# TensorE's order written out and bound by dependencies in a gated-recurrence and maxout-FFN kernel

## The chip, the cores and the metric

The kernel runs on one core of a Trainium2 chip. The metric is the device time of one execution in microseconds (us). Most executions of one kernel agree within 1%.

## The reference, cut to what matters

A linear recurrence with a complex gate for each channel (4 batches, 8 heads, 768 steps, head size 48), whose output goes through a feed-forward block with a maximum of three projections.

```python
mag = np.sqrt(a_re * a_re + a_im * a_im)
scale = np.minimum(mag, 0.999) / (mag + 1e-06)        # gate, limited in size
...
for t in range(S):
    new_re = ar * S_re - ai * S_im
    new_im = ar * S_im + ai * S_re
    S_re, S_im = (new_re + kv, new_im)                # kv = k[t] outer v[t]
    y[:, :, t] = np.einsum('bhd,bhde->bhe', q[:, :, t], S_re)
...
h = np.maximum(np.maximum(x @ w1, x @ w2), x @ w3)    # 3072 x 384 by 384 x 768
return h @ w_out
```

## The kernel before

Tokens are taken in tiles of 128 and groups of two tiles; there are twelve groups. The names in the profile are these:

- Gates of the *next* group, in three steps on ScalarE, VectorE and GpSimd: logarithms of size (`Ln`) and half-angle tangents (`w`). ScalarE's table functions are bound to each other in the order in which the program emits them:

```python
def tab(ins):
    if "tab" in T:
        tc.add_manual_dep(ins.ins, T["tab"].ins.name, order, reason="table order")
    T["tab"] = ins

def act(**kw):
    tab(nc.scalar.activation(**kw))
...
def s2():                                             # the last gate step
    L, w, e, ar, ai = part("L"), part("w"), part("e"), part("ar"), part("ai")
    nc.scalar.activation(out=e, in_=ar, func=AF.Abs)
    nc.vector.tensor_tensor(out=w, in0=w, in1=e, op=OP.add)
    act(out=L, in_=w, func=AF.Ln)
    act(out=L, in_=L, func=AF.Exp, scale=-1.0)
    (nc.gpsimd if g > 1 else nc.vector).tensor_tensor(out=ai, in0=ai, in1=L, op=OP.mult)
    nc.vector.tensor_tensor(out=w, in0=w, in1=L, op=OP.mult)
    nc.vector.scalar_tensor_tensor(out=w, in0=w, scalar=2.0, in1=ai, op0=OP.subtract, op1=OP.mult)
    nc.scalar.activation(out=ar, in_=ar, func=AF.Sign, bias=tiny)
    nc.scalar.activation(out=ai, in_=ar, func=AF.Copy, scale=-0.25, bias=0.25)
    nc.scalar.activation(out=ar, in_=ar, func=AF.Copy, scale=-1.0 / math.pi)
```

- Angles: after two sums (`mds`, one a tile, each followed by two Exps and GpSimd's products into k and q) comes a table load, Arctan of `w`, two VectorE products, and the cumulative sums `cs` on TensorE; then sines.

```python
def turns(g, cs, meanwhile):
    act(out=w[:, lo:hi], in_=w[:, lo:hi], func=AF.Arctan)
    nc.vector.tensor_tensor(out=w[:, lo:hi], in0=w[:, lo:hi], in1=ar[:, lo:hi], op=OP.mult)
    nc.vector.tensor_tensor(out=w[:, lo:hi], in0=w[:, lo:hi], in1=ai[:, lo:hi], op=OP.add)
    meanwhile(2)                                      # two steps of the FFN
    for c in cs:
        ...
        nc.tensor.matmul(out=ps, lhsT=upto, rhs=w[:, c * DM:(c + 1) * DM], start=True, stop=c == 0)
```

- A tile: transposes (`tp`), factors of decay (`F`), products with them on VectorE (`Q`, `KB`, `QB`, `QG`), score products `A` and `B`, state products `dk`, suffix sums (`sfx`), outputs `y`. FFN: `up` and `op`.

The order of emission is woven from streams. The compiler's scheduler may then put the instructions of an engine in another order, as it does in e1 below:

```python
return [call(scores, x, "A"), call(gather, x, "A"), call(scores, x, "B")] + tr[:1] \
    + [call(gather, x, "B"), call(state, x)] + tr[1:] + ct + pr[:1] + kt \
    + [call(outputs, x, tokens(x))] + pr[1:]
...
weave((0.0, 1.0, tile_steps(g * C) + tile_steps(g * C + 1)), (0.0, 0.7, pre_steps(g + 1, feed)),
      (0.0, 1.0 if g > 1 else 0.5, [call(feed, 1) for _ in ffn]))
```

Of the kernel before, what the change touches and what calls it, by code (L numbers as in the profile page):

```python
# [45 lines left out]
def kernel(  # L46
# [52 lines left out]
# [5 lines that stand above are left out]

    def act(**kw):
        tab(nc.scalar.activation(**kw))  # L106

    def table(nm):
        tab(nc.scalar.preload_act_table_set(nm))
# [240 lines left out]
    def turns(g, cs, meanwhile):  # L350

        lo, hi = cs[0] * DM, (cs[-1] + 1) * DM
        w, ar, ai = T["w", g], flat(T["ar", g]), flat(T["ai", g])
# [3 lines that stand above are left out]
        meanwhile(2)  # L357
        for c in cs:
            ps = psM.tile([P, DM], FP, tag="mm", padded_shape=[P, 512], name="cs")
            nc.tensor.matmul(out=ps, lhsT=upto, rhs=w[:, c * DM:(c + 1) * DM], start=True, stop=c == 0)  # L360
            if c > 0:
                nc.tensor.matmul(out=ps, lhsT=every, rhs=w[:, 0:DM], start=False, stop=True)
            t = nat2.tile([P, DM], FP, tag="t", name="t")
            nc.scalar.activation(out=t, in_=ps, func=AF.Copy, bias=MAGIC)
            nf = nat2.tile([P, DM], FP, tag="nf", name="nf")
            nc.vector.scalar_tensor_tensor(out=nf, in0=t, scalar=MAGIC, in1=ps, op0=OP.subtract, op1=OP.subtract)
            T["nf", g * C + c] = nf
            if c == C - 1 and (g + 1) % GB > 0:
                T["carry", g + 1] = nat1.tile([1, DM], FP, tag="carry", name="carry")
                nc.scalar.dma_start(out=T["carry", g + 1], in_=nf[P - 1:P])  # L370
# [29 lines left out]
    def products(x):  # L400
        g, c = divmod(x, C)

        def sums(mat, nm):
            ps = psM.tile([P, DM], FP, tag="mm", padded_shape=[P, 512], name=nm)
            nc.tensor.matmul(out=ps, lhsT=mat, rhs=T["Ln", g][:, c * DM:(c + 1) * DM], start=True, stop=True)  # L405
            return ps

        def s0():

            ps = sums(mid, "mds")  # L410
            for nm, sg in (("k", 1.0), ("q", -1.0)):
                E = nat2.tile([P, DM], FP, tag="E", name="E")
                act(out=E, in_=ps, func=AF.Exp, scale=sg)
                eng = nc.gpsimd if g > 1 else nc.vector
                eng.tensor_tensor(out=hd(T[nm, x]), in0=E, in1=hd(T[nm, x]), op=OP.mult)  # L415

        def s1():
            for nm in "kq":
                u = T["U" + nm, x] = us[nm][x % len(us[nm])]
                nc.vector.tensor_tensor(out=u[:, :, :, 0:D], in0=T["CS", x], in1=two(hd(T[nm, x])), op=OP.mult)  # L420

        def s2():

            ps = sums(rest, "sfx")
            En = nat2.tile([P, DM], FP, tag="E", name="En")
            act(out=En, in_=ps, func=AF.Exp, scale=-1.0)
            u = T["Uk", x][:, :, :, 0:D]
            nc.vector.tensor_tensor(out=u, in0=u, in1=two(En), op=OP.mult)

        return s0, s1, s2  # L430


    def turn(x, hg):
        if hg == 0:
            T["K", x] = un2.tile([P, H, P], FP, tag="K", name="K")

            T["Q", x] = un2.tile([P, 4 * H, 48], FP, tag="Q", name="Q")
        hs = slice(hg * HU, (hg + 1) * HU)
        for nm in "kq":
            tp = psM.tile([P, HU, P], FP, tag="mm", padded_shape=[P, 4, P], name="tp")  # L440
            for j in range(HU):
                nc.tensor.transpose(out=tp[0:DD, j], in_=both(T["U" + nm, x], hg * HU + j), identity=ident)  # L442
            if nm == "k":
                nc.scalar.copy(out=T["K", x][0:DD, hs], in_=tp[0:DD])  # L444
            else:
                nc.scalar.copy(out=T["Q", x][0:DD, 4 * hg * HU:4 * (hg + 1) * HU, 0:32],
                               in_=tp[0:DD].rearrange("p j (c t) -> p (j c) t", c=4))

    def cut(x):
        g, c = divmod(x, C)  # L450
        F = T["F", x] = fs[x % 2]
        ps = psM.tile([P, HU, NF], FP, tag="mm", padded_shape=[P, 4, P], name="F")
        for h in range(H):
            o = h % 2 * L64
            nc.tensor.matmul(out=ps[o:o + D, h // 2], lhsT=T["Ln", g][:, c * DM + h * D:c * DM + (h + 1) * D],  # L455
                             rhs=cuts, start=True, stop=True)

        for o in (0, L64):
            for h in range(2):
                act(out=F[o:o + D].rearrange("p (i h) n -> p i h n", h=2)[:, :, h], in_=ps[h * L64:h * L64 + D],  # L460
                    func=AF.Exp, scale=-1.0)
# [35 lines left out]
    def scores(x, nm):  # L497

        ps = psS.tile([P, 2, 512], FP, tag="s", name=nm)
        for h in range(H):  # L500
            for o in range(0, P, 32):
                c, j = divmod(o // 32, 2)
                if nm == "A":
                    nc.tensor.matmul(out=ps[o:o + 32, 0, h * 48:(h + 1) * 48], lhsT=T["K", x][0:DD, h, o:o + 32],  # L504
                                     rhs=T["Q", x][0:DD, 4 * h + 2 * c + j], start=True, stop=True)
                else:
                    nc.tensor.matmul(out=ps[o:o + 32, h // HU, h % HU * P:h % HU * P + 80],  # L507
                                     lhsT=T["KB", x][0:DD, h, o:o + 32],
                                     rhs=T["QB", x][0:DD, 2 * h + c, 16 * j:16 * j + 80], start=True, stop=True)
        T[nm, x] = ps  # L510
# [28 lines left out]
    def state(x):  # L539
# [8 lines left out]
        for h in range(H):  # L548
            o = h % 2 * (P - D)
            for lo, hi in ((0, L64), (L64, DD)):  # L550
                for c in range(2):
                    r = slice(c * L64, (c + 1) * L64)
                    nc.tensor.matmul(out=ps[lo:hi, c, h * D:(h + 1) * D], lhsT=both(T["Uk", x], h)[r, lo:hi],  # L553
                                     rhs=T["v", x][r, c, h // 2, o:o + D], start=True, stop=True)
        dk = ps[0:DD, :, 0:DM].rearrange("p c (i u d) -> p c i u d", u=2, d=D)
        G = T["G", x]
# [9 lines left out]
    def outputs(x, xs):  # L566
# [10 lines left out]
        for todo in zip(*queues):  # L577
            for r, c, i, n, new, start, stop in todo:
                h, lo = 2 * i + n // 2, 32 * n
                nc.tensor.matmul(out=y[32 * (r % 4):32 * (r % 4) + 32, r // 4, c * L64:(c + 1) * L64],  # L580
                                 lhsT=V[:, c, i, lo:lo + 32] if new else G[0:DD, c, i, lo:lo + 32],
                                 rhs=atm[:, h] if new else QG[0:DD, 2 * h + c], start=start, stop=stop)
        if x == xs[0]:
# [7 lines left out]
    def up_step(xs, fp, i):  # L591
# [7 lines left out]
        for j in range(2):  # L599
            f = 2 * fp + j  # L600
            for d in range(KD):
                nc.tensor.matmul(out=ps[:, j], lhsT=ws[i][:, d, f * P:(f + 1) * P], rhs=xT[:, d],  # L602
                                 start=(d == 0), stop=(d == KD - 1))
        if i == 0:
            nc.scalar.copy(out=dst, in_=ps)  # L605
# [3 lines left out]
    def out_step(xs, x):  # L609
        hT, o = T["hT", xs[-1]], (x - xs[0]) * P  # L610
        ps = psM.tile([P, DM], FP, tag="mm", padded_shape=[P, 512], name="op")
        for f in range(KF):
            nc.tensor.matmul(out=ps, lhsT=hT[:, f, o:o + P], rhs=wo[:, f], start=(f == 0), stop=(f == KF - 1))  # L613
        ot = fp2.tile([P, DM], FP, tag="ot", name="ot")
        nc.scalar.copy(out=ot, in_=ps)  # L615
        nc.sync.dma_start(out=out[x * P:(x + 1) * P, :], in_=ot)


    def call(f, *a):
        return lambda: f(*a)  # L620
# [71 lines left out]
    load(2, load_a, load_kq)  # L692


    held = []
    for g in range(1, NG):
        load(g + 1, load_v)
        load(g + 2, load_a, load_kq)
        ffn = held + ffn_steps(tokens(g * C - 1))
        held = [ffn.pop()]  # L700

        def feed(n):
            for _ in range(min(n, len(ffn))):
                ffn.pop(0)()

        if g > 1:
            feed(1)
        weave((0.0, 1.0, tile_steps(g * C) + tile_steps(g * C + 1)), (0.0, 0.7, pre_steps(g + 1, feed)),
              (0.0, 1.0 if g > 1 else 0.5, [call(feed, 1) for _ in ffn]))
    for f in held + ffn_steps(tokens(NX - 1)):  # L710
        f()

# [29 lines left out]
```

## Time and profile before

| | |
|---|---|
| time | 724.0 us (median of 3; 722.6 to 724.2) |
| span of the profiled run | 719.9 us |
| granted TensorE clock, mean | 0.974 |
| TensorE, VectorE, ScalarE, GpSimd busy | 90%, 72%, 56%, 17% |
| first A of the third group to first A of the last, nine groups | 165.2 to 639.2 us, 52.7 us each |

A "group time" below is this distance. The prediction shows the lines and how they are read. In a line of the order of time, the first number is the start in us and the second the time from the first start to the last end; since matmuls overlap (in the prediction's lines 36 ups last 7.93 us, and the next matmul starts after 7.77), I take distances between starts. In a line of waits the numbers are: total us, times, longest.

### The profile page before, as it was taken

The numbers are of one execution on the slowest core, as the hardware profiler recorded it, in microseconds if no ns is written. First come the engines' busy times: TensorE is split into PE (matmuls) and PEld (weight loads), VectorE is DVE, ScalarE is ACT, GpSimd is POOL, SyncE is SP. The second block draws the span as 40 slices with busy tenths as digits, with TensorE's granted clock in tenths as the row PEclk, the third lists the DMA queues.
The fourth block names the chain that finished last, engine by engine and source line by source line (L and its number), as shares of the span: only waits on it lengthen the run. The fifth ranks groups of instructions, "written<-read, shape, count | busy, mean of one in ns | idle before, by whom it ended". The sixth has DMA issues, their size and how long they took to land.

```text
span 719.9 us, 22988 instructions
## 1 busy us (share of the span) xinstructions
PE 649.9 (90%) x10308; PEld 505.3 (70%) x10308; DVE 515.7 (72%) x718; ACT 400.3 (56%) x677; POOL 120.6 (17%) x121
## 2 busy tenths in 40 slices
PE   1256678779999999999999999999999999999997
PEld 0144567657877878878778778878778778778785
DVE  6999998867856867867856867867857858755210
ACT  6778665666556556556556656566466465422000
POOL 9300000601301302202203103104004004000000
PEclk9987799979999999999999999999999999999999
DMA  9780442040320320330320320410410210000000
GB/s 226 218 191 15 95 126 46 13 89 24 57 60 21 57 63 18 57 68 14 66 67 5 73 63 4 87 47 9 94 36 13 46 36 2 2 25 2 14 11 22
DMA packets 134178, 39.23 MB, mean 54 GB/s; under 512 B 126784, under 2 KB 129856, under 8 KB 134080
## 3 DMA queue, kind: packets, MB, share of 16 engines
q1 hardware_dynamic: 133824, 37.76, 23.7%
q8 instruction: 80, 1.31, 0.8%
q14 instruction: 18, 0.15, 0.1%
q10 hardware_dynamic: 256, 0.01, 0.0%
HBM read 33.03 MB, written 4.72 MB: 52 GB/s over the span
## 4 chain that ended last, share of the span: by engine, by line
PE 69%; issue 14%; DVE 8%; ACT 6%; DMA 2%; POOL 1%; SPq 0%; DVEq 0%; ACTq 0%; POOLq 0%
PE up L602 31%; PE op L613 13%; PE tp L442 5%; PE y L580 5%; PE dk L553 3%; PE B L507 2%; ACT CS L106 2%; PE sfx L405 2%; PE F L455 2%; PE cs L360 2%; PE mds L405 2%; PE A L504 2%; DVE uq L420 1%; ACT af L376 1%; DVE QG L469 1%
## 5 line engine op out<-in xcount | busy, mean ns | idle before, releaser
L602 PE MATMUL up<-xT,w 128*128 128x256 f32 (+1 forms) x1404 | 297.2, 365 | 0.6 <-ACT xT L588 0.6
L602 PEld LDWEIGHTS up<-xT,w 128*128 128x128 f32 x1404 | 246.6, 190 | 36.2 <-ACT xT L588 1.1
L613 PE MATMUL op<-wo,hT 128*128 128x384 f32 x288 | 98.5, 491 | 4.0 <-DVE wo L292 4.0
L469 DVE TENSOR_TENSOR Q<-Q,f 112x512 f32<-112x512 f32 x48 | 40.8, 851 | 75.3 <-ACT f L106 75.2
L338 POOL TENSOR_TENSOR ai<-ai,L 128x768 f32<-128x768 f32 x10 | 25.8, 2577 | 357.3 <-ACT L L106 328.1
L607 DVE TENSOR_TENSOR hT<-hT,up 128x512 f32<-128x512 f32 (+1 forms) x78 | 49.9, 641 | 43.0 <-PE up L602 42.9
L613 PEld LDWEIGHTS op<-wo,hT 128*128 128x128 f32 x288 | 52.8, 190 | 37.2 <-issue 3.6
L605 ACT COPY hT<-up 128x512 f32<-128x512 f32 (+1 forms) x39 | 21.4, 549 | 72.9 <-PE up L602 72.7
L444 ACT COPY K<-tp 112x512 f32<-112x512 f32 x48 | 27.8, 579 | 40.8 <-PE tp L442 40.5
L615 ACT COPY ot<-op 128x384 f32<-128x384 f32 x24 | 11.5, 480 | 67.8 <-PE op L613 67.8
L580 PEld LDWEIGHTS y<-atm,vb 128*32 128x32 f32 x1536 | 39.3, 111 | 12.7 <-issue 8.5
L106 ACT ACTIVATE f<-F 48x296 f32<-48x296 f32 x96 | 39.7, 413 | 15.0 <-PE F L455 14.1
L580 PE MATMUL y<-atm,vb 128*32 128x64 f32 x1536 | 46.7, 223 | 1.4 <-DVE hT L607 1.4
L580 PE MATMUL y<-QG,g 112*32 112x64 f32 x1536 | 46.2, 221 | 0.0
L469 DVE TENSOR_TENSOR QB<-Q,f 112x512 f32<-112x512 f32 (+1 forms) x48 | 44.5, 966 | 0.0
L405 PE MATMUL mds<-Ln,mid 128*128 128x384 f32 x48 | 24.0, 584 | 19.0 <-POOL cuts L120 14.8
L507 PE MATMUL B<-QB,KB 112*32 112x80 f32 x1536 | 32.9, 238 | 8.8 <-DVE QB L469 8.6
L580 PEld LDWEIGHTS y<-QG,g 112*32 112x32 f32 x1536 | 39.9, 111 | 0.5 <-issue 0.5
L415 POOL TENSOR_TENSOR k<-E,k 128x384 f32<-128x384 f32 x20 | 28.9, 1444 | 68.2 <-ACT E L106 68.2
L507 PEld LDWEIGHTS B<-QB,KB 112*32 112x32 f32 x1536 | 28.1, 112 | 16.0 <-issue 14.5
L442 PE MATMUL tp<-ident,uk 128*112 128x128 f32 x192 | 32.3, 293 | 7.7 <-DVE uk L420 7.7
L360 PE MATMUL cs<-w,upto 128*128 128x384 f32 x48 | 21.8, 585 | 17.7 <-DVE w L356 17.7
(111 smaller groups left out, 1078.3 us busy)
## 6 DMA issues: line engine op xcount, KB each, us to landing
ar<-in_a_re_dram SPq DMA_DIRECT2D x24, 192.0 KB, 3.3
ai<-in_a_im_dram SPq DMA_DIRECT2D x24, 192.0 KB, 3.9
k<-in_k_dram SPq DMA_DIRECT2D x24, 192.0 KB, 3.5
q<-in_q_dram SPq DMA_DIRECT2D x24, 192.0 KB, 3.3
vb<-in_v_dram SPq DMA_DIRECT2D x96, 48.0 KB, 2.4
out_dram<-ot SPq DMA_DIRECT2D x24, 192.0 KB, 1.9
raw<-in_moe_w_dram SPq DMA_DIRECT2D x5, 768.0 KB, 6.5
raw<-in_moe_w_out_dram SPq DMA_DIRECT2D x3, 768.0 KB, 4.2
```

Source lines behind the costliest of these rows:

```text
L106: tab(nc.scalar.activation(**kw))
L360: nc.tensor.matmul(out=ps, lhsT=upto, rhs=w[:, c * DM:(c + 1) * DM], start=True, stop=c == 0)
L405: nc.tensor.matmul(out=ps, lhsT=mat, rhs=T["Ln", g][:, c * DM:(c + 1) * DM], start=True, stop=True)
L415: eng.tensor_tensor(out=hd(T[nm, x]), in0=E, in1=hd(T[nm, x]), op=OP.mult)
L442: nc.tensor.transpose(out=tp[0:DD, j], in_=both(T["U" + nm, x], hg * HU + j), identity=ident)
L444: nc.scalar.copy(out=T["K", x][0:DD, hs], in_=tp[0:DD])
L469: nc.vector.tensor_tensor(out=out, in0=in_, in1=f.to_broadcast([DD, H, 2 * n, 8]), op=OP.mult)
L507: nc.tensor.matmul(out=ps[o:o + 32, h // HU, h % HU * P:h % HU * P + 80], lhsT=T["KB", x][0:DD, h, o:o + 32], rhs=T["QB", x][0:DD, 2 * h + ...
L580: nc.tensor.matmul(out=y[32 * (r % 4):32 * (r % 4) + 32, r // 4, c * L64:(c + 1) * L64], lhsT=V[:, c, i, lo:lo + 32] if new else G[0:DD, c ...
L602: nc.tensor.matmul(out=ps[:, j], lhsT=ws[i][:, d, f * P:(f + 1) * P], rhs=xT[:, d], start=(d == 0), stop=(d == KD - 1))
L607: nc.vector.tensor_tensor(out=dst, in0=dst, in1=ps, op=OP.max)
L613: nc.tensor.matmul(out=ps, lhsT=hT[:, f, o:o + P], rhs=wo[:, f], start=(f == 0), stop=(f == KF - 1))
```

## The change

Its intent is to save switches of TensorE's array between shapes (in the kernel before, the last up ahead of B or dk takes 309 ns from start to start, an up ahead of another 216): A and B side by side, the state products beside the factors of decay, FFN steps between. Every matmul and transpose from the third group on is bound to the one before it; the second group gets the new order of emission without the binding.

```diff
+    def chained(f):
+        def g(**kw):
+            ins = f(**kw)
+            if "chain" in T:
+                if T["chain"] is not None:
+                    tc.add_manual_dep(ins.ins, T["chain"].ins.name, order, reason="TensorE's order")
+                T["chain"] = ins
+            return ins
+        return g
+
+    mm, mt = chained(nc.tensor.matmul), chained(nc.tensor.transpose)
 ... (all nc.tensor.matmul become mm, all nc.tensor.transpose mt)
-        weave((0.0, 1.0, tile_steps(g * C) + tile_steps(g * C + 1)), (0.0, 0.7, pre_steps(g + 1, feed)),
-              (0.0, 1.0 if g > 1 else 0.5, [call(feed, 1) for _ in ffn]))
+        if g > 1:
+            feed(1)
+        pairs(x)             # A, B, then what is gathered from them
+        gates[0]()
+        feed(1)              # one step of the FFN
+        turned(y)            # transposes of the next tile
+        gates[1]()
+        ahead(x)             # dk, F, sfx, first products
+        feed(1)
+        sums[0]()            # mds and its Exps
+        outputs(x, tokens(x))
+        rest(y)              # KB, QB, QG
+        gates[2]()           # the last gate step
+        feed(1)
+        sums[1]()
+        turning()            # table load, Arctan, two FFN steps, cs, sines
+        pairs(y)
+        units[0]()
+        feed(1)
+        units[1]()
+        feed(1)
+        turned(y + 1)
+        ahead(y)
+        feed(1)
+        outputs(y, tokens(y))
+        rest(y + 1)
+        feed(len(ffn))
+
+    for g in range(1, NG):
+        if g == 2:
+            T["chain"] = None
+        group(g)
```

More of the change, by code (lines that the diff above doesn't have):

```diff
@@ L359, in turns @@
             ps = psM.tile([P, DM], FP, tag="mm", padded_shape=[P, 512], name="cs")
-            nc.tensor.matmul(out=ps, lhsT=upto, rhs=w[:, c * DM:(c + 1) * DM], start=True, stop=c == 0)
+            mm(out=ps, lhsT=upto, rhs=w[:, c * DM:(c + 1) * DM], start=True, stop=c == 0)
             if c > 0:
-                nc.tensor.matmul(out=ps, lhsT=every, rhs=w[:, 0:DM], start=False, stop=True)
+                mm(out=ps, lhsT=every, rhs=w[:, 0:DM], start=False, stop=True)
             t = nat2.tile([P, DM], FP, tag="t", name="t")
@@ L404, in sums @@
             ps = psM.tile([P, DM], FP, tag="mm", padded_shape=[P, 512], name=nm)
-            nc.tensor.matmul(out=ps, lhsT=mat, rhs=T["Ln", g][:, c * DM:(c + 1) * DM], start=True, stop=True)
+            mm(out=ps, lhsT=mat, rhs=T["Ln", g][:, c * DM:(c + 1) * DM], start=True, stop=True)
             return ps
@@ L441, in turn @@
             for j in range(HU):
-                nc.tensor.transpose(out=tp[0:DD, j], in_=both(T["U" + nm, x], hg * HU + j), identity=ident)
+                mt(out=tp[0:DD, j], in_=both(T["U" + nm, x], hg * HU + j), identity=ident)
             if nm == "k":
@@ L454, in cut @@
             o = h % 2 * L64
-            nc.tensor.matmul(out=ps[o:o + D, h // 2], lhsT=T["Ln", g][:, c * DM + h * D:c * DM + (h + 1) * D],
+            mm(out=ps[o:o + D, h // 2], lhsT=T["Ln", g][:, c * DM + h * D:c * DM + (h + 1) * D],
                              rhs=cuts, start=True, stop=True)
@@ L503, in scores @@
                 if nm == "A":
-                    nc.tensor.matmul(out=ps[o:o + 32, 0, h * 48:(h + 1) * 48], lhsT=T["K", x][0:DD, h, o:o + 32],
+                    mm(out=ps[o:o + 32, 0, h * 48:(h + 1) * 48], lhsT=T["K", x][0:DD, h, o:o + 32],
                                      rhs=T["Q", x][0:DD, 4 * h + 2 * c + j], start=True, stop=True)
                 else:
-                    nc.tensor.matmul(out=ps[o:o + 32, h // HU, h % HU * P:h % HU * P + 80],
+                    mm(out=ps[o:o + 32, h // HU, h % HU * P:h % HU * P + 80],
                                      lhsT=T["KB", x][0:DD, h, o:o + 32],
@@ L552, in state @@
                     r = slice(c * L64, (c + 1) * L64)
-                    nc.tensor.matmul(out=ps[lo:hi, c, h * D:(h + 1) * D], lhsT=both(T["Uk", x], h)[r, lo:hi],
+                    mm(out=ps[lo:hi, c, h * D:(h + 1) * D], lhsT=both(T["Uk", x], h)[r, lo:hi],
                                      rhs=T["v", x][r, c, h // 2, o:o + D], start=True, stop=True)
@@ L579, in outputs @@
                 h, lo = 2 * i + n // 2, 32 * n
-                nc.tensor.matmul(out=y[32 * (r % 4):32 * (r % 4) + 32, r // 4, c * L64:(c + 1) * L64],
+                mm(out=y[32 * (r % 4):32 * (r % 4) + 32, r // 4, c * L64:(c + 1) * L64],
                                  lhsT=V[:, c, i, lo:lo + 32] if new else G[0:DD, c, i, lo:lo + 32],
@@ L601, in up_step @@
             for d in range(KD):
-                nc.tensor.matmul(out=ps[:, j], lhsT=ws[i][:, d, f * P:(f + 1) * P], rhs=xT[:, d],
+                mm(out=ps[:, j], lhsT=ws[i][:, d, f * P:(f + 1) * P], rhs=xT[:, d],
                                  start=(d == 0), stop=(d == KD - 1))
@@ L612, in out_step @@
         for f in range(KF):
-            nc.tensor.matmul(out=ps, lhsT=hT[:, f, o:o + P], rhs=wo[:, f], start=(f == 0), stop=(f == KF - 1))
+            mm(out=ps, lhsT=hT[:, f, o:o + P], rhs=wo[:, f], start=(f == 0), stop=(f == KF - 1))
         ot = fp2.tile([P, DM], FP, tag="ot", name="ot")
@@ L695, with group @@
     held = []
-    for g in range(1, NG):
+    def group(g):
+        x, y = g * C, g * C + 1
         load(g + 1, load_v)
         load(g + 2, load_a, load_kq)
-        ffn = held + ffn_steps(tokens(g * C - 1))
-        held = [ffn.pop()]
+        ffn = held + ffn_steps(tokens(x - 1))
+        held[:] = [ffn.pop()]
         def feed(n):
@@ L704, in feed, with pairs, ahead, turned @@
                 ffn.pop(0)()
+        pre = pre_steps(g + 1, feed) if g + 1 < NG else [lambda: None] * 8
+        gates, sums, (turning,), units = pre[:3], pre[3:5], pre[5:6], pre[6:]
+        def pairs(x):
+            for f in (scores, gather):
+                for nm in "AB":
+                    f(x, nm)
+        def ahead(x):
+            state(x)
+            if x + 1 < NX:
+                cut(x + 1)
+                products(x + 1)[2]()
+                prep(x + 1, 0)
+        def turned(x):
+            if x < NX:
+                turn(x, 0)
+                turn(x, 1)
+        def rest(x):
+            if x < NX:
+                for p in range(1, 4):
+                    prep(x, p)
         if g > 1:
             feed(1)
-        weave((0.0, 1.0, tile_steps(g * C) + tile_steps(g * C + 1)), (0.0, 0.7, pre_steps(g + 1, feed)),
-              (0.0, 1.0 if g > 1 else 0.5, [call(feed, 1) for _ in ffn]))
+        pairs(x)
[27 more added lines that the diff above has]
+        group(g)
     for f in held + ffn_steps(tokens(NX - 1)):
```

## The prediction

The sum of the forecast is 724 - 9 for the switches + 5 for cs = 720 us. The added work in front of cs is 1.9 + 0.7 = 2.6 us, and what takes it to "up to 3 us" was my estimate for `ai`. "Drain", there and in the expectation of e9, stands for the longer distance from start to start where the shape changes: 149 ns from dk to tp in the kernel before, 15 on average within dk. What TensorE does in that time is not shown.

> **What bounds the kernel now.** I began with the page: busy times, then the forty slices.
>
> ```profile
> PE 649.9 (90%) x10308; PEld 505.3 (70%) x10308; DVE 515.7 (72%) x718; ACT 400.3 (56%) x677; POOL 120.6 (17%) x121
> ...
> PE   1256678779999999999999999999999999999997
> ...
> DVE  6999998867856867867856867867857858755210
> ```
>
> TensorE reads 9 in every slice from about 170 us on, and VectorE reads 5 to 8 there; before about 110 us it is VectorE that reads 9. So there are two regimes. Next I asked for busy time by stretch, cutting at the first score product A of a group (two 128-token tiles).
>
> ```profile
> 111.00:165.00 54.00, 43.64 (x842) 34.66 (x842) 43.37 (x59) 34.05 (x58) 11.71 (x6) 0.91 0.28 52
> 165.20:218.00 52.80, 52.62 (x851) 40.85 (x850) 38.13 (x52) 31.38 (x53) 9.58 (x6) 1.00 0.23 47
> 323.20:376.00 52.80, 52.62 (x851) 40.85 (x850) 38.23 (x52) 31.48 (x53) 9.10 (x6) 1.00 0.23 46
> ```
>
> The columns are: stretch, its length, then busy us (and count) of TensorE, weight loads, VectorE, ScalarE, GpSimd, then clock and DMA. The second group (111 to 165) leaves TensorE 10 us idle. From the third group on each takes 52.8 us, TensorE is busy for 52.62 of it, and the clock is full. Ten such groups, a front of 165 us and a tail make 720 us. "Busy" does not mean "at its peak", so I read start-to-start distances in TensorE's order of time.
>
> ```profile
> 396.61 7.93 PE L602 MATMUL up<-xT,w 128*128 128x256 f32 x36
> 404.38 1.45 PE L360 MATMUL cs<-w,upto 128*128 128x384 f32 x4
> 405.67 0.81 PE L362 MATMUL cs<-w,every 128*128 128x384 f32 x2
> 406.41 0.89 PE L504 MATMUL A<-Q,K 112*32 112x48 f32 x64
> 407.23 2.86 PE L602 MATMUL up<-xT,w 128*128 128x256 f32 x12
> 410.01 1.31 PE L507 MATMUL B<-QB,KB 112*32 112x80 f32 x64
> 411.26 0.65 PE L442 MATMUL tp<-ident,uk 128*112 128x128 f32 x4
> 411.84 0.32 PE L553 MATMUL dk<-vb,uk 64*64 64x48 f32 x6
> ```
>
> In a run, 36 up-projection matmuls take 404.38 - 396.61 = 7.77 us, 0.216 each. Twelve of them between A and B take 410.01 - 407.23 = 2.78 us, where 12 x 0.216 is 2.59. That 0.19 us is the price of switching the array's shape. The chain of waits shows no TensorE wait over 0.4 us in the steady groups; the large ones, as the 17.7 us of cs on w, fall in the front. So TensorE gains nothing there by waiting less, only by switching less.
>
> [...] the last full-array up before B or dk takes 309 ns start to start, not 216. [...] the 112x1024 product KB takes 1.22 us alone and 2.03 us beside GpSimd's k and q products.
>
> **The change, part by part.** No operation is added or removed[...].
>
> *A with B.* Both run at 112 rows by 32 columns, so B behind A needs no switch. Leaving A costs 136 ns start to start (11 within A), entering B 93 ns (309 - 216). Saved: 0.125 + 0.093 = 0.22 us a tile, 0.44 a group. The slow first ups after A are then behind B, and I count nothing for them.
>
> *dk with F.* The two do not have the same shape (64 rows by 64 or 48 columns against 128 by 48), so I expect a drain between them still, about the 0.15 us that dk to tp takes now. Entering F (0.093) is saved and the exit is not: 0.1 us a tile; if there were no drain, 0.23. A group: 0.2 to 0.45.
>
> *dk no longer split.* In some groups the scheduler put six of dk's matmuls between two transposes. These groups take 52.80 us, the others 52.44. About half have it: 0.2 us a group.
>
> The sum is 0.84 to 1.1 us a group; adding every distance of the new order from its present neighbours gives 51.8 against 52.7. Over ten groups 8 to 11 us, so 713 to 716 us if no wait is added.
>
> *What moves.* The written order also fixes when the angle sums cs come, and they hang from a long chain on other engines. Now the stretch from F to cs is 336.39 to 351.58, 15.2 us. In the new order it is F, sfx, up, mds, y, up, mds, two ups, cs: the same members and the same 15.2 us. But the first mds moves behind sfx and an up (3.4 us later after F), the second behind an up (2.6 us later), and the last gate step is emitted after the first mds, while ScalarE's table functions are bound in the order of emission. Its Ln and Exp now run long before F. So within the 15.2 us the chain must run: mds lands at 4.7; two Exps, Ln and Exp to 7.3; GpSimd's k and q products, then ai (2.58 us) to 10.3; VectorE's w to 11.3; the table load (1.28) after the second mds's Exps to 12.3; Arctan 0.85 to 13.2; two VectorE products of 0.95 to 15.1. That is break-even with nothing else in the way. But VectorE is not free there:
>
> ```profile
> 339.49 2.03 DVE L469 TENSOR_TENSOR KB<-K,f 112x1024 f32<-112x1024 f32 x1
> ...
> 346.74 2.02 DVE L469 TENSOR_TENSOR QG<-Q,f 112x1024 f32<-112x1024 f32 x1
> 348.68 0.67 DVE L607 TENSOR_TENSOR hT<-hT,up 128x512 f32<-128x512 f32 x1
> 349.28 0.94 DVE L355 TENSOR_TENSOR w<-w,ar 128x768 f32<-128x768 f32 x1
> 350.26 0.96 DVE L356 TENSOR_TENSOR w<-w,ai 128x768 f32<-128x768 f32 x1
> ```
>
> It is busy without a pause from 338.9 to 351.2, so w is ready only 0.4 us before cs starts at 351.58. The change brings into this window two gate products (1.9 us), one more max of 0.7 and GpSimd's ai[...]. If VectorE takes all that before w, cs waits up to 3 us; if it slips w forward, nearly nothing. I take 0.3 to 3 us, in the middle 1.5, in the nine groups that compute angles for a next one: 3 to 27 us, middle 13.
>
> *The second group* gets the new order of emission but no binding. VectorE has 43 us of work in 54 there; it may end a few us earlier or later, and I see no reason for either: 0 +- 4.
>
> **The rivals.** (1) Fewer switches only: 714 us, 1.3% faster. For it: the steady groups have no wait and all distances repeat to the nanosecond. Against: the thin slack at cs. (2) A wait at cs takes the place of the switches: up to 742 us. For it: 0.4 us of slack against 3 us of added work. Against: the work on VectorE is 38 us in 52.8, so a delay is absorbed once in each group, and the up steps before cs were probably counted so that it is ready. (3) Another engine becomes the bound: no, none has over 38 us of 52.8. (4) A score buffer: A and B now take both large PSUM buffers at once, and dk needs one. It comes 4.5 us after B, while the two copies out of A take 0.73 + 0.43; hidden. (5) Transfers: at 23% of the DMA engines, hidden anyway.
>
> **Range and chances.** 724 - 9 for switches, plus 0 to 13 for cs with the smaller end likelier, since the order was written with intent: I choose +5, so **720 us**. Eight times in ten between 710 and 734. Faster by over 2% needs under 709.5, which means all switches saved, no wait, and some 5 us from the second group: 0.11. Slower by over 2% needs over 738.5, so over 2.5 us of waiting in every group: 0.08. Within 2%: 0.81.
>
> **What would show it.** Right on switches: A straight before B, with 12 to 20 ns between them, and a third group onward of 51.5 to 52 us where there is no wait. Wrong there: dk to F at over 0.25 us. Right on the wait: a TensorE wait of cs for VectorE's w (about nine times, 0.3 to 3 us each), with VectorE busy in front of it. What would make it wrong as a whole: a wait elsewhere in the bound order, such as y on the sums of the state or transposes on uk, in every group; or a second group that ends over 5 us earlier or later.

## The result, and the profile after

The changed kernel takes **793.6 us** (median of 4; 792.8 to 794.3) against 724.1 us (722.6 to 726.2). The ratio of times is 1.096, 95% interval 1.093 to 1.099. Ratios here are the mean time of one kernel's fast runs over that of the other's in the same rounds, so not quite the ratio of the medians.

From the page of the changed kernel, busy times and TensorE's clock in forty slices:

```profile
PE 663.8 (84%) x10308; PEld 520.9 (66%) x10308; DVE 513.4 (65%) x718; ACT 394.0 (50%) x677; POOL 111.9 (14%) x121
...
PEclk9976978799899899899899899899899899799999
```

No engine has more work than before to speak of, but every share fell: the time is idle time. And the clock, which in the kernel before stood at 9 (90% or more) in each slice of the steady stretch, now dips once in about every three slices, which is once in a group.

TensorE's waits between the third group's start and the last group's, first of the changed kernel:

```profile
PE cs L111 <- DVE w L369: 55.4, 9, 6.9
```

The kernel before has in its same stretch only this (all matmuls of the changed kernel bear line 111, that of the helper):

```profile
PE tp L442 <- DVE uq L420: 1.1, 6, 0.2
```

Nine waits, one in each group that computes angles for a next one, 6 us each, all of cs for w. One of them in TensorE's order of time, changed kernel, fifth group:

```profile
299.25 1.14 PE L111 MATMUL dk<-vb,uk 64*64 64x48 f32 x64
300.31 0.72 PE L111 MATMUL F<-cuts,Ln 128*48 128x74 f32 x16
...
310.33 5.34 PE L111 MATMUL up<-xT,w 128*128 128x256 f32 x24
321.73 2.90 PE L111 MATMUL cs<-w,upto 128*128 128x384 f32 x4 [6.06 <-DVE w L369]
324.42 1.17 PE L111 MATMUL cs<-w,every 128*128 128x384 f32 x2
325.53 0.89 PE L111 MATMUL A<-Q,K 112*32 112x48 f32 x64
326.23 1.29 PE L111 MATMUL B<-QB,KB 112*32 112x80 f32 x64
```

The 24 ups need 24 x 0.216 = 5.2 us, so TensorE stood ready for cs at 315.5 and began at 321.73: 6.2 us. Then cs took 325.53 - 321.73 = 3.8 us (4.1 in most groups) where the kernel before needs 2.03. The clock tells why. Busy time by stretch (the eighth column is the clock):

```profile
310.30:315.50 5.20, 5.20 (x25) 4.37 (x23) 5.20 (x5) 1.69 (x3) 1.81 (x2) 1.00 0.12 20
315.60:321.70 6.10, 0.07 (x1) 0.00 (x0) 2.42 (x3) 3.99 (x6) 2.40 (x3) 0.72 0.05 8
321.70:325.50 3.80, 3.77 (x6) 1.85 (x6) 0.56 (x1) 0.49 (x1) 0.00 (x0) 0.55 1.06 193
```

It falls during the wait and is at 0.55 while cs runs. Cut finer, the clock is 1.00 from 315.5 to 318.3 and 0.50 from 318.3 to 321.7: in this group it falls when TensorE has been idle for some 2.7 us. In the nine groups it falls 2.3 to 5.2 us into the wait. In five of the nine groups the half clock lasts into A too, which then takes 1.2 to 1.3 us instead of 0.70.

From the two traces, a group takes 60.0 us on average (172.4 to 712.8 us, nine groups) where it took 52.7. That is +7.38. In means of the nine: +6.32 for the wait (6.2 in eight groups, 7.0 in the last), +1.94 for the slow cs, +0.33 for the slow A behind it, and -1.24 for switches, as e2 below shows them without the wait; 7.35 together. Nine groups make +66.4; the front, up to the third group's A, is 7.2 us longer (172.4 against 165.2) and the rest 1.0 shorter (79.8 against 80.8). Sum +72.6, as the spans: 792.6 - 719.9 = 72.7. The front is only placed here, not explained.

Why is w so late? The other engines between F and cs, in the same group. VectorE first:

```profile
306.61 3.43 DVE L482 TENSOR_TENSOR QB<-Q,f 112x512 f32<-112x512 f32 x2
309.97 2.83 DVE L482 TENSOR_TENSOR QG<-Q,f 112x1024 f32<-112x1024 f32 x1
312.72 0.95 DVE L352 TENSOR_TENSOR w<-w,L 128x768 f32<-128x768 f32 x1
...
314.06 0.94 DVE L353 SCALAR_TENSOR_TENSOR w<-w,ai 128x768 f32<-128x768 f32 x1
...
319.16 0.96 DVE L368 TENSOR_TENSOR w<-w,ar 128x768 f32<-128x768 f32 x1 [3.56 <-ACT w L106]
320.04 0.68 DVE L620 TENSOR_TENSOR hT<-hT,up 128x512 f32<-128x512 f32 x1
320.64 0.95 DVE L369 TENSOR_TENSOR w<-w,ai 128x768 f32<-128x768 f32 x1
```

Then GpSimd:

```profile
307.53 1.44 POOL L428 TENSOR_TENSOR q<-E,q 128x384 f32<-128x384 f32 x1
308.93 2.79 POOL L351 TENSOR_TENSOR ai<-ai,L 128x768 f32<-128x768 f32 x1
```

Then ScalarE:

```profile
313.75 0.85 ACT L329 ACTIVATE L<-ai 128x768 f32<-128x768 f32 x1 [5.75 <-issue]
314.50 0.47 ACT L106 ACTIVATE E<-mds 128x384 f32<-128x384 f32 x1
315.03 0.84 ACT L356 ACTIVATE ai<-ar 128x768 f32<-128x768 f32 x1
315.78 0.47 ACT L106 ACTIVATE E<-mds 128x384 f32<-128x384 f32 x1
316.15 0.83 ACT L357 ACTIVATE ar<-ar 128x768 f32<-128x768 f32 x1
316.99 1.28 ACT L122 ACT_TABLE_LOAD   x1
318.29 0.84 ACT L106 ACTIVATE w<-w 128x768 f32<-128x768 f32 x1
```

These lines show a relay. GpSimd's `ai` ends at 311.7 because it had to follow the k and q products (q ends at 308.97). VectorE makes `w` (line 353) only at 315.0, behind QB and QG, which are slow here beside GpSimd (the two QB 3.43 us and QG 2.83; 1.82 and 1.22 in a group's second half, where GpSimd is idle). On ScalarE the two Exps of the second `mds`, whose matmuls end at 310.5, come late: a square for the following group's gates (line 329) writes `L`, which VectorE reads until 313.7, and stands ahead of them. ScalarE's copy into `ai` (line 356) may not start before VectorE has read `ai` (it starts at 315.03, VectorE's product ends at 315.00), and in ScalarE's queue the second Exp of `mds`, another copy and the table load stand behind it; so Arctan starts at 318.3 though its input is there at 315.0. The load takes 1.28 us and nothing idles around it: the copy ahead of it ends at 316.98, the load at 318.27, and Arctan starts at 318.29. And a max of the FFN falls between the two last products.

### The profile page after: what moved, and what is told of

The parts are those of the page before. It is cut to its first block, busy times and chain, and to the rows that moved or that the text cites. A ratio compares the mean times of both kernels' runs of the same rounds, so it can differ in the third digit from the quotient of the medians.

```text
span 792.6 us, 22981 instructions
## 1 busy us (share of the span) xinstructions
PE 663.8 (84%) x10308; PEld 520.9 (66%) x10308; DVE 513.4 (65%) x718; ACT 394.0 (50%) x677; POOL 111.9 (14%) x121
## 5 line engine op out<-in xcount | busy, mean ns | idle before, releaser
L111 PE MATMUL cs<-w,upto 128*128 128x384 f32 x48 | 34.3, 868 | 70.8 <-DVE w L369 70.8
L111 PEld LDWEIGHTS op<-wo,hT 128*128 128x128 f32 x288 | 55.2, 193 | 41.6 <-issue 5.9
L111 PEld LDWEIGHTS cs<-w,upto 128*128 128x128 f32 x48 | 14.1, 323 | 83.0 <-issue 66.0
L482 DVE TENSOR_TENSOR QB<-Q,f 112x512 f32<-112x512 f32 (+1 forms) x48 | 59.1, 1269 | 0.0
L577 DVE TENSOR_TENSOR g<-g,dk 112x384 f32<-112x384 f32 x40 | 22.1, 553 | 48.7 <-PE dk L111 48.1
L529 DVE COPY_PREDICATED atm<-maskd,A 128x512 f32<-128x512 uint8 x24 | 17.9, 744 | 52.8 <-PE A L111 52.8
L482 DVE TENSOR_TENSOR Q<-Q,f 112x512 f32<-112x512 f32 x48 | 33.0, 688 | 18.2 <-ACT f L106 18.0
L482 DVE TENSOR_TENSOR QG<-Q,f 112x1024 f32<-112x1024 f32 x24 | 43.7, 1821 | 0.0
L377 ACT ACTIVATE t<-cs 128x384 f32<-128x384 f32 x24 | 11.8, 490 | 59.1 <-PE cs L111 59.1
```

Source lines behind the costliest of these rows:

```text
L111: ins = f(**kw)
L377: nc.scalar.activation(out=t, in_=ps, func=AF.Copy, bias=MAGIC)
L482: nc.vector.tensor_tensor(out=out, in0=in_, in1=f.to_broadcast([DD, H, 2 * n, 8]), op=OP.mult)
L529: nc.vector.copy_predicated(out=out, mask=mask, data=data)
L577: nc.vector.tensor_tensor(out=new, in0=new, in1=dk[:, c], op=OP.add)
```

## The experiments

My theory, **"chain"**: the new order of *emission* puts the last gate step behind the first sums. Since ScalarE's table functions are bound in that order, its Ln and Exp, and with them the whole relay up to cs, come late. The binding of TensorE is innocent. The rival, **"binding"**: a fixed order on TensorE costs the time by itself, and a scheduler that is free would go round the waits. A third question is whether fewer switches save what I had worked out.

Group times in the table are from the profiled run, from the third group's A to the last one's; "wait" is the start of cs less the end of the work ahead of it, and "cs" its length.

| run | time us | ratio to before (95%) | group us | wait us | cs us |
|---|---|---|---|---|---|
| before | 724.1 | | 52.7 | 0 | 2.0 |
| after | 793.6 | 1.096 (1.093 to 1.099) | 60.0 | 6.2 | 3.6 to 4.1 |
| e1, not bound | 783.2 | 1.081 (1.078 to 1.083) | 59.2 | 5 | 3.6 to 4.1 |
| e2, gate step early | 722.0 | 0.996 (0.993 to 0.999) | 52.1 | 0.3 | 2.1 |
| e3, four ups ahead of cs | 728.1 | 1.004 (1.001 to 1.007) | 52.7 | 1.0 | 2.1 |
| e4, before, bound | 724.6 | 1.000 (0.997 to 1.004) | 52.7 | 0 | 2.0 |
| e5, e2 with front as before | 718.5 | 0.991 (0.988 to 0.993) | 52.1 | 0.3 | 2.1 |
| e6, e5 with sums early | 719.4 | 0.993 (0.991 to 0.995) | 52.3 | 0.4 | 2.1 |
| e7, Ln and Exp free | 731.0 | 1.008 (1.004 to 1.012) | 52.1 | 0.3 | 2.1 |
| e8, A with B alone | 720.6 | 0.994 (0.991 to 0.997) | 52.4 | 0 | 2.0 |
| e9, dk with F alone | 733.6 (one run) | | 53.4 | 0 | 2.0 |
| e10, ScalarE cleared | 766.3 | 1.054 (1.048 to 1.059) | 56.9 | 3.3 | 2.8 to 4.1 |
| e12, e5 with three ups | 716.4 | 0.988 (0.985 to 0.990) | 51.8 | 0 | 2.0 |

**e1: the order of emission without the binding.**

```diff
     for g in range(1, NG):
-        if g == 2:
-            T["chain"] = None
         group(g)
```

> The changed kernel with its order of emission, but TensorE's instructions not bound to it. Theory 'chain' (the new order of emission puts the last gate step and the angle sums' ScalarE and GpSimd work too late, so cs waits 6.2 us in each of nine groups and then runs 2.1 us longer at a lower clock): the compiled order of TensorE is nearly the same, cs only slips behind A and nine matmuls of B (about 1 us), so 775 to 795 us. Rival 'binding' (the fixed order itself costs the time, a free scheduler would avoid the waits): back to about 724 us.

It is nearly as slow. TensorE's order of time in one of its groups:

```profile
312.48 0.58 PE L111 MATMUL B<-QB,KB 112*32 112x80 f32 x18
317.91 2.90 PE L111 MATMUL cs<-w,upto 128*128 128x384 f32 x4 [4.85 <-DVE w L369]
```

The free scheduler slipped cs behind A and the first 18 matmul instructions of B (nine products; each is two instructions), and it still waits 4.85 us. So the binding is not the cause. That w was ready there in the scheduler's reckoning is my inference from the order that it chose.

**e4: the kernel before, bound to its own order of emission.** The helper of the change is added to the kernel before, with `T["chain"] = None` at the third group; nothing is reordered.

> The kernel before with its own order of emission, but TensorE's instructions bound to it from the third group on. Theory 'chain': the bound order is almost the one that the scheduler chose, so 720 to 730 us. Rival 'binding': well over 740 us.

The binding alone costs nothing that 0.4% would show. With e1 this rejects "binding" from both sides.

**e2: the last gate step early, TensorE's order unchanged.**

```diff
         gates[1]()
+        gates[2]()
         ahead(x)
 ...
         rest(y)
-        gates[2]()
         feed(1)
```

> The changed kernel with the last gate step emitted straight after the second one, ahead of the state products, instead of after the outputs; TensorE's order stays bound and is the same. Theory 'chain': the wait of cs falls from 6.2 us to 0 to 1.5 us and the clock stays up, a group takes 52 to 53.5 us, the whole 722 to 735 us. Rival 'binding': 785 to 795 us as before.

One line moved gives back 72 us. GpSimd's `ai` now runs 15 us ahead of the k product instead of behind it, and cs starts 0.3 us after the ups (24 x 0.216 = 5.2 us after 292.45); first GpSimd, then TensorE:

```profile
272.25 2.58 POOL L351 TENSOR_TENSOR ai<-ai,L 128x768 f32<-128x768 f32 x1 [28.45 <-ACT L L106]
...
287.85 1.84 POOL L428 TENSOR_TENSOR k<-E,k 128x384 f32<-128x384 f32 x1 [10.08 <-ACT E L106]
```

```profile
292.45 5.34 PE L111 MATMUL up<-xT,w 128*128 128x256 f32 x24
297.94 1.53 PE L111 MATMUL cs<-w,upto 128*128 128x384 f32 x4
```

Most groups take 51.8 us. This still holds 0.3 us of wait and 0.1 of a slower cs (2.10 us against 2.03), so the new order itself takes 51.4.

**e7: the gate step left late, but its Ln and Exp taken out of the table order.** Data alone keeps them ahead of Arctan; in the compiled order they do run before the table load, so the result is right.

```diff
-            act(out=L, in_=w, func=AF.Ln)
-            act(out=L, in_=L, func=AF.Exp, scale=-1.0)
+            nc.scalar.activation(out=L, in_=w, func=AF.Ln)
+            nc.scalar.activation(out=L, in_=L, func=AF.Exp, scale=-1.0)
```

> The changed kernel as it is, but the Ln and the Exp of the last gate step are not bound into the order of ScalarE's table functions (data alone keeps them ahead of Arctan). TensorE's order is the changed kernel's. Theory 'chain through the table order': they then run before the group's first product, as in e2, so the wait of cs falls from 6.2 us to under 0.5 and the time to 720 to 725 us. Rival (VectorE's and GpSimd's load in the stretch is what makes w late, wherever the gate step is): over 750 us.

The steady groups behave as in e2: 51.8 us, wait 0.3. So it is the order of the *table functions* through which the place of emission acts. The expected whole was missed: 731 us, because the second group became longer (65.4 us from A to A against 58.3 in the changed kernel). The edit holds for the first groups too; I did not follow that further.

**e3: four up steps ahead of cs instead of two.**

```diff
-        meanwhile(2)
+        meanwhile(4 if "chain" in T else 2)
```

> The changed kernel with four up-projection steps ahead of cs instead of two (from the third group on), fewer later. Theory 'chain': the chain is as late as it was, but 5.2 of its 6.2 us are covered, and with a short wait the clock stays up: 793.6 - 9 x (5.2 + 2.1) = 728 us, 724 to 742. Rival 'it comes back elsewhere' (the steps are missed later, y then waits for the state or tp for uk): over 760 us.

As expected to the microsecond: nothing on the chain is changed, but TensorE has 5.2 us more to do ahead of cs, the rest of the wait is 1.0 us, and with it so short the clock stays up (cs 2.1 us). Of the 1.0 us, 0.2 falls between the ups and 0.8 just before cs. The line names ScalarE's copy of an up result, which frees a PSUM buffer at 253.42, as what came last. But w itself is there only at 253.28 (VectorE's last product, 0.95 us from 252.33), so without the copy cs would start 0.14 us sooner at most.

```profile
253.43 1.53 PE L111 MATMUL cs<-w,upto 128*128 128x384 f32 x4 [0.64 <-ACT hT L618]
```

**e10: gate step late, but ScalarE's queue cleared ahead of Arctan.** The scaled signs go to `e`, so they need not wait for VectorE, and the next group's square of `ai` is bound in the table order.

```diff
-            nc.scalar.activation(out=L, in_=ai, func=AF.Square)
+            act(out=L, in_=ai, func=AF.Square)
 ...
-            nc.scalar.activation(out=ai, in_=ar, func=AF.Copy, scale=-0.25, bias=0.25)
+            nc.scalar.activation(out=e, in_=ar, func=AF.Copy, scale=-0.25, bias=0.25)
 ... (the carry and turns() then use e in place of ai)
```

> The changed kernel, gate step still late, but with ScalarE's queue cleared ahead of Arctan: the scaled signs go to another buffer, so that they don't wait for VectorE's w, and the next group's square of a_im is bound behind this group's table functions. Theory: of the 6.2 us of waiting some 3.7 come from ScalarE's order (ai copy, second Exp, ar copy and table load run after w, and a max falls between the two last products) and 2.5 from the late gate step with VectorE's and GpSimd's load. So cs waits 2.5 us; if so short a wait leaves the clock up, a group takes 54.3 us and the whole 741 us; if the clock falls all the same, 760. Rival (ScalarE's order is not on the path): over 785 us.

```profile
371.93 1.59 PE L111 MATMUL cs<-w,upto 128*128 128x384 f32 x4 [3.15 <-DVE w L369]
```

The wait falls from 6.2 to 3.3 us (in eight of the nine groups; 8.5 us from the first of 24 ups to cs, less 5.2), where I had expected 2.5. The table load now runs before w is ready, and no max stands between the two products. From the end of w (line 353) to the end of the last product it takes 2.9 us (368.9 to 371.8) instead of 6.6 (315.0 to 321.6): the 3.7 that I had put down to ScalarE's order. But w itself comes 0.8 us later after the first Exp than in the changed kernel, since a product into `g` now falls beside GpSimd's k product and takes 1.35 us instead of 0.55. So the net gain is 2.9. The work behind the wait was slower in these groups too: cs takes 2.8 to 4.1 us. In the group shown it takes 2.80, and A behind it 1.29; the mean clock is 1.00 from 363.9 to 372.0 and 0.64 from 372.2 to 376.0, so it fell after cs had begun. The whole came to 766 us, not 760.

**e8: A with B alone, in the bound kernel before.** The tile's steps emit both score products, then both gathers, in the place of A; the freed places stay empty.

> The kernel before, bound to its own order as e4, with B emitted straight after A and nothing else changed. Theory 'switches': a group takes 0.44 us less than in e4 (52.75 us on average there), so 52.3, and the whole 719 to 721 us. Rival (no switch is saved): 724 to 726 us.

720.6 us against 724.6 of e4. Where no wait comes in, a group takes 51.89 us against 52.43, so 0.54 saved; in the other groups the transposes after the first up step wait up to 0.8 us and 0.22 is left.

**e9: dk with F alone, in the bound kernel before.** dk moves from ahead of the second pair of transposes to just before F. This was one run without rounds, so its whole time decides nothing; the profile does.

> The kernel before, bound to its own order as e4, with F emitted straight behind the state products dk. Theory 'switches': dk to F still drains (0.15 us), so only the entry of F is saved, 0.1 us a tile, 0.2 us a group: 52.5 us on average against 52.75 in e4, if no wait comes in. Rival (no gain, or a loss): 52.7 us or more.

dk to F takes as long as dk to a transpose did (1.07 us from dk's first to what follows), so the exit from dk is not saved. But the two pairs of transposes now stand closer together and wait for a PSUM buffer that ScalarE's copy frees (0.82 us in one place), and a group takes 53.4 us. Alone, this part loses.

**e5 and e6: towards a better kernel.** e5 is e2 with the second group woven as in the kernel before. e6 also emits the second `mds` ahead of its up step.

```diff
+        if g == 1:
+            weave((0.0, 1.0, tile_steps(x) + tile_steps(y)), (0.0, 0.7, pre_steps(2, feed)),
+                  (0.0, 0.5, [call(feed, 1) for _ in ffn]))
+            return
```

> The early gate step of e2, and the second group woven as in the kernel before (new order from the third group on only). Theory 'chain and front': the third group then starts at about 165 us as in the kernel before instead of 169 us, groups keep their 51.8 us, so 716 to 719 us, against 722 of e2. Rival (the 4 us of the front are lost with the new order of the third group, or are chance): 721 to 724 us.

> As e5, with the second tile's sum matmul (mds) in front of the up step that it stood behind, so that the second table load and Arctan start 2.6 us earlier. Theory 'chain': what is left of the wait of cs, 0.24 us in most groups, goes; 51.55 us a group, 1 to 3 us less than e5. Rival: same as e5 within 1 us.

e5 is at 718.5 us, as expected, but in its profiled run the third group starts at 168.2 us, not 165, so only part of the gain is placed. e6 gains nothing: the wait stays at 0.4 us. After the early gate step the second `mds` is no longer what w waits for.

**e12: e5 with three up steps ahead of cs.** `meanwhile(3 if "chain" in T else 2)`.

> As e5 with three up steps ahead of cs instead of two from the third group on, to cover what is left of its wait (0.3 us in a group, 3 us in the front). Theory: 51.55 us a group, 714 to 717 us. Rival (the step is missed later, or there is nothing left to cover): 718 to 721 us.

716.4 us, 1.2% below the kernel before and the best version here. TensorE reaches cs without a wait. Groups take 51.77 us, not 51.55: the transposes now take 2.0 us instead of 1.84, twice a group.

## Why the prediction was right or wrong

- **Wrong as a whole.** It forecast 720 us in 710 to 734, with 0.08 for slower by over 2%; measured 793.6.
- **What bounds the kernel: right.** TensorE's order of time had no slack but the switches, and a wait could come only from the chain to cs.
- **Switches: right, and a little small.** The parts said 0.84 to 1.1 us a group and the sum of distances 51.8 us. e2, e5 and e7 do show 51.8 in most groups, but 0.3 of it is wait and 0.1 a slower cs, so that this agreement is luck: the new order takes 51.4, 1.2 less than before. Six of the nine groups before took 52.8, not "about half", which leaves that part at 0.2. Start to start, A to B is 23 ns (12 to 20 expected) and dk to F 148 ns, the 0.15 us that I had assumed. Taken alone, A with B saved 0.22 to 0.54 a group (e8).
- **"What moves": the right wait, half of the reason, the wrong size.** The step that failed is "I take 0.3 to 3 us, in the middle 1.5", and under it "the table load (1.28) after the second mds's Exps to 12.3". The wait measured 6.2, and the table load ended at 18.0. Relative to F's start (300.31), the chain was to end at 15.1 us with nothing in the way; it ended at 321.59, so 21.3. Term by term: Ln and Exp end at 7.3, as written. GpSimd's `ai` ends at 11.4, not 10.3 (+1.1, its products are slower beside VectorE: q takes 1.44 us, 0.98 at 317.01, where VectorE is idle). VectorE's w ends at 14.7, not 11.3 (another +2.3, behind QB and QG). These 3.4 us are the "up to 3" that I allowed. What I left out is ScalarE's own queue: I let the table load end at 12.3, in time for Arctan, but it stood behind a copy that waits until VectorE has made w, so Arctan ended at 18.8 instead of 1.9 us after w (+2.2), and the max between the last products added 0.6. e10 takes these two out, and with them the 1.0 us that my sum had left between w and Arctan: 3.7 us less behind w, 2.9 net.
- **The clock: a missing term.** I priced a wait by its length alone. At 3.3 us (e10, cs 2.8 to 4.1 us) and 6.2 (3.6 to 4.1) the work behind it was slower as well; at 1.0 us (e3) and 0.3 (e2) it was not (2.1). In the changed kernel that is 2.3 us a group on average, 1.9 in cs and 0.3 in A. Nine groups at 6.3 + 2.3 us cost 77 us, of which the switches gave 11 back.
- **The reason given for the smaller end was no evidence.** "The order was written with intent" moved my middle from 13 us of waiting to 5. The thin slack at cs, which I had read and named, spoke against it.
- **Second group "0 +- 4": a little outside in the profiled run.** A to A it took 58.3 us, not 53.7; with the old weave it took 52.7 to 55.2 in the runs with an early gate step (e5, e6, e12). Its start differs by 4 us between the profiled runs of the kernel before and of e4, in which the code ahead of it is the same (111.5 and 115.6), so how much of it is the order stays open.
- **Rivals (3) and (5): right.** No engine became the bound and no transfer shows. On (4), dk never waited for a score buffer after the front.

## What to carry to other kernels

When an order is written out for one engine, write the relay that feeds its rarest input for each of the other queues too, in order, with what each entry waits for: an entry that is ready can stand behind one that isn't (here ScalarE's Exp of `mds`, whose matmuls end at 310.5, behind a square that started at 313.75). Look for orders that are bound already, as ScalarE's table functions here; moving an emission moves them with it, and one moved line was worth 72 us (e2 and e7 put 6 us a group on it). And price a long TensorE wait with the slower clock behind it: waits of 3.3 and 6.2 us were followed here by a cs of 2.8 to 4.1 us instead of 2.0.
